# Attention, MLP and gated MLP in one kernel: the opening's order is written out by hand

## The chip, the cores and the metric

The kernel runs on one core of a Trainium2 chip, as one program. The metric is the device time of one execution in microseconds (us). Differences under 0.2% are not told from no change.

## What is computed

Three stages run one after another for a batch of 8, 576 positions and 512 model columns, all in float32:

```python
# 1 attention over 32 memory slots, 8 heads of 64
a = exp(phi - max(phi, axis=2)); a = a / (sum(a, axis=2) + 1e-9)
k_m, v_m = a^T k, a^T v                       # per head: 32 x 64
attn = softmax(q k_m^T / 8);  x = attn v_m    # heads side by side: 576 x 512
# 2 MLP with layer norm, 512 -> 2048 -> 512
x = x + relu(layernorm(x) * g_ln @ w_ch1) @ w_ch2
# 3 gated MLP with a mix over positions
h = gelu(x @ w_in); u, v = halves(h)
out = x + (u * (w_sg @ (layernorm(v) * g) + b_sg)) @ w_out
```

The weights arrive as float64 and are turned into float32 on the chip. A product that needs float32 exactness is made of three matmuls on fp32r parts: high by high, high by low, low by high.

## The kernel before

**Stages.** `phase1` does attention and the first MLP for the eight batches, `phase2` the gated MLP. This change is in the first batch of `phase1`.

**Preparing a batch.** `load_phi`, `load_kv`, `load_rem` and `load_q` fetch phi, k, v and q. The 64 positions past 512 are loaded on their own, as `prz` (phi) and `kvr` (k and v). `prep_red` and `prep_max` find the column maxima, `prep_exp` subtracts and exponentiates, `prep_sum` sums over positions, `prep_kv` makes k_m and v_m (`kvp`), `prep_norm` divides (`kvn`), and `prep_T` turns them (`ptk`, `kvT`).

**Queries.** Three groups of query tiles belong to batch 0: tiles 0 and 1, tiles 2 and 3, and the half tile 4. For each, `t_q` turns q (`ptq`, `qT`), `t_scores` makes scores (`sc`) and their exponentials (`z`), `t_norm` divides, and `t_attn` writes the high and low part of the attention weights (`aTh`, `aTl`). `t_x` makes attention's output (`px`, `x`), which only the residual and the layer norm need.

**W1 and W2.** w_ch1 is used in four quarters of 512 columns, each four raw tiles of 128 x 512 float64. `to_f32` converts a raw tile with one ScalarE and two VectorE instructions (lines 112 to 114). `scale_w1` multiplies by the layer norm's weight (`wc`), `center_w1` takes off the column mean (the matmuls `cm`, then line 510), and `make_vw` and `evict_vw` multiply by v_m (`pvw`, `vw`). w_ch2 is 16 raw tiles; `split_w2` converts each and cuts it into `whl`, the low part on GpSimd.

**The MLP's steps.** A step is `m1`, six matmuls from attention weights and `vw` to hidden columns (`ph`, cut into `hh` and `hl`), and `m2`, six matmuls of 512 columns from those with `whl` into `py`. The first batch has two blocks of positions, of 256 and 320. It takes quarter 0 in steps 0 to 3 (first block) and 4 to 7 (second), quarter 1 in steps 8 to 15, and so on. `m2` follows `m1` by `LAG` = 3 steps.

**Order.** `at_time` files each piece of work under a time in steps, and the list is worked off by time. The tile framework then orders each engine's queue by its own estimate of when work is ready, so that the order in the code is not the order on the engines. All DMAs are issued by SyncE (line 85).

Of the kernel before, what the change touches and what calls it, by code (L numbers as in the profile page):

```python
# [26 lines left out]

@with_exitstack
def fused_kernel(ctx: ExitStack, tc: tile.TileContext, q, k, v, phi, g1, w1, w2, w_in, g2, w_sg, b_sg, w_out, out):
    nc = tc.nc  # L30
# [71 lines left out]

    def to_f32(raw, gate=None):

        words = raw.bitcast(U32).rearrange("p (n two) -> p n two", two=2)
        lo, hi = words[:, :, 0], words[:, :, 1]

        gates = ExitStack()
        for ins in gate or ():
            gates.enter_context(tc.issue_after(ins.ins))  # L110
        with gates:
            A.activation(hi.bitcast(F32), hi.bitcast(F32), AF.Prelu, scale=2.0 ** -112, alpha=-(2.0 ** 32))
            V.tensor_scalar(lo, lo, 29, None, op0=ALU.logical_shift_right)
            V.scalar_tensor_tensor(out=lo, in0=hi, scalar=3, in1=lo, op0=ALU.logical_shift_left, op1=ALU.bitwise_or)
        return lo.bitcast(F32)
# [27 lines left out]
    def phase1():  # L143
# [142 lines left out]
        def prep_sum(b):  # L286
            ph, pr = st["phi", b]
            sm = at.tile([P, H, NM], F32, tag="kvn", name="sm")
            G.tensor_tensor(out=sm, in0=ph[:, :, 0, :], in1=ph[:, :, 1, :], op=ALU.add)
            for c in (2, 3):  # L290
                G.tensor_tensor(out=sm, in0=sm, in1=ph[:, :, c, :], op=ALU.add)
            for g in range(2):
                rows, sub = slice(REM * g, REM * g + REM), slice(4 * g, 4 * g + 4)
# [835 lines left out]
```

## Time and profile before

| | |
|---|---|
| time, median of 3 runs (lowest to highest) | 1200.78 us (1200.47 to 1202.09) |
| the profiled execution: time, span | 1204.2 us, 1202.3 us |
| busy: TensorE (PE), VectorE (DVE), ScalarE (ACT), GpSimd (POOL) | 97%, 58%, 39%, 33% of the span |
| TensorE's mean granted clock | 0.989 of full speed |

The shares are means over the whole span. In the profile, PEclk is the granted clock of TensorE as a share of its full 2.4 GHz, and 0.50 is its other level, 1.2 GHz. "SPq" is SyncE's queue, which issues the DMAs.

### The profile page before, as it was taken

The page shows a single profiled execution, that of the slowest core. Times are in us where ns is not written, and L with a number is a line of the kernel's source. Part 1 is how long each engine was busy: PE and PEld are TensorE (multiplying, and loading weights), DVE is VectorE, ACT ScalarE, POOL GpSimd, SP SyncE. Part 2 cuts the span into 40 slices and gives each one's busy share as a digit, 9 for nine tenths or more (in the row PEclk, how much of TensorE's full clock was granted, in tenths as well). Part 3 has the DMA queues.
Part 4 walks back from the last instruction along what each step waited for, and adds up shares of the span by engine and source line. Part 5 has one row for each costly group of instructions (what it writes and reads, how often), then busy time and mean ns, then how long its engine had stood idle before and what let it go on. Part 6 is the DMA issues. An engine that isn't in the chain of part 4 may idle for free.

```text
span 1202.3 us, 20687 instructions
## 1 busy us (share of the span) xinstructions
PE 1168.9 (97%) x7711; PEld 992.1 (83%) x7711; DVE 692.3 (58%) x1669; ACT 466.6 (39%) x1071; POOL 402.4 (33%) x622
## 2 busy tenths in 40 slices
PE   4899999999999999999999999999999999999998
PEld 2487678888788888788888888889989988998997
DVE  4886765645644645644546445567476377447532
ACT  3754423322322322422333445445444354344430
POOL 2233302311201211201211112456666475566641
PEclk8799999999999999999999999999999999999999
DMA  8976544552341551341400343032240042022201
GB/s 251 382 224 176 154 108 117 139 161 55 102 117 27 151 133 49 102 125 27 124 27 19 107 131 111 27 82 88 81 140 18 19 153 66 2 85 83 79 19 71
DMA packets 198900, 124.14 MB, mean 103 GB/s; under 512 B 93072, under 2 KB 174096, under 8 KB 198800
## 3 DMA queue, kind: packets, MB, share of 16 engines
q1 hardware_dynamic: 198800, 122.82, 35.4%
q8 instruction: 61, 1.00, 0.4%
q14 instruction: 39, 0.32, 0.1%
HBM read 99.72 MB, written 31.33 MB: 109 GB/s over the span
## 4 chain that ended last, share of the span: by engine, by line
PE 88%; DVE 6%; DMA 2%; SPq 1%; issue 1%; ACT 1%; POOL 1%; POOLq 0%; DVEq 0%; ACTq 0%
PE ph L596 16%; PE py L628 11%; PE py L626 11%; PE py L627 10%; PE pvs L1034 8%; PE po L1057 8%; PE pv L925 8%; PE pu L1009 7%; PE pvw L548 2%; SPq L85 1%; PE kvp L321 1%; PE cm L508 1%; PE sc L407 1%; PE px L463 1%; PE px L465 1%
## 5 line engine op out<-in xcount | busy, mean ns | idle before, releaser
L596 PE MATMUL ph<-aTh,vw 128*128 128x320 f32 (+1 forms) x1024 | 248.8, 300 | 3.0 <-DVE hl L583 1.7
L626 PE MATMUL py<-whl,hh 128*128 128x512 f32 x512 | 202.0, 395 | 2.9 <-ACT hh L582 2.9
L596 PEld LDWEIGHTS ph<-aTh,vw 128*128 128x128 f32 x1024 | 178.7, 189 | 30.3 <-issue 9.5
L627 PE MATMUL py<-whl,hh 128*128 128x512 f32 x512 | 201.3, 393 | 0.0
L628 PE MATMUL py<-whl,hl 128*128 128x512 f32 x512 | 182.0, 396 | 0.0
L583 DVE SCALAR_TENSOR_TENSOR hl<-ph,hh 128x256 fp32r<-128x256 f32 x256 | 106.3, 420 | 98.9 <-ACT hh L582 98.3
L582 ACT ACTIVATE hh<-ph 128x256 fp32r<-128x256 f32 x256 | 97.0, 385 | 167.5 <-PE ph L596 121.2
L596 PE MATMUL ph<-aTl,vw 128*128 128x256 f32 (+1 forms) x512 | 152.8, 298 | 0.0
L1034 PE MATMUL pvs<-wsh,vhl 128*128 128x288 f32 x576 | 121.0, 295 | 0.0
L626 PEld LDWEIGHTS py<-whl,hh 128*128 128x128 f32 x512 | 96.1, 188 | 25.3 <-ACT hh L582 6.1
L627 PEld LDWEIGHTS py<-whl,hh 128*128 128x128 f32 x512 | 96.3, 188 | 19.5 <-issue 1.1
L1009 PE MATMUL pu<-yTh,whl 128*128 128x288 f32 x512 | 111.0, 296 | 0.4 <-DVE ug L914 0.4
L596 PEld LDWEIGHTS ph<-aTl,vw 128*128 128x128 f32 x512 | 97.1, 190 | 12.2 <-issue 4.3
L628 PEld LDWEIGHTS py<-whl,hl 128*128 128x128 f32 x512 | 89.9, 189 | 10.9 <-issue 1.6
L1034 PEld LDWEIGHTS pvs<-wsh,vhl 128*128 128x128 f32 x576 | 94.4, 188 | 0.6
L925 PE MATMUL pv<-whl,yTh 128*128 128x512 f32 x288 | 91.0, 396 | 0.0
L1057 PE MATMUL po<-whl,gh 128*128 128x512 f32 x288 | 90.0, 391 | 0.0
L1009 PEld LDWEIGHTS pu<-yTh,whl 128*128 128x128 f32 x512 | 85.4, 189 | 1.9 <-DVE ug L914 0.8
L582 ACT ACTIVATE cr<-ph 128x64 fp32r<-128x64 f32 x128 | 28.5, 225 | 146.9 <-PE ph L596 146.5
L430 POOL TENSOR_TENSOR z<-z,r 128x512 f32<-128x512 f32 (+2 forms) x18 | 17.0, 943 | 180.1 <-DVE r L429 130.5
L1037 POOL TENSOR_TENSOR gt<-gt,ug 128x288 f32<-128x288 f32 x64 | 52.9, 827 | 68.6 <-DVE gt L1036 65.8
L1034 PE MATMUL pvs<-wsl,vhl 128*128 128x288 f32 x256 | 75.6, 295 | 0.0
(154 smaller groups left out, 2226.6 us busy)
## 6 DMA issues: line engine op xcount, KB each, us to landing
raw<-in_moe_w_ch_dram SPq DMA_DIRECT2D x32, 512.0 KB, 7.5
wc<-w_d SPq DMA_DIRECT2D x28, 512.0 KB, 5.7
y_d<-x SPq DMA_DIRECT2D x36, 256.0 KB, 2.3
yt<-y_d SPq DMA_DIRECT2D x36, 256.0 KB, 2.7
yr<-y_d SPq DMA_DIRECT2D x36, 256.0 KB, 2.8
kv<-in_k_dram SPq DMA_DIRECT2D x32, 256.0 KB, 3.9
kv<-in_v_dram SPq DMA_DIRECT2D x32, 256.0 KB, 4.4
out_dram<-yr SPq DMA_DIRECT2D x32, 256.0 KB, 2.0
```

The source lines that it names most:

```text
L548: mm = PE.matmul(ps[g][ms, :], vT[rs_, ms], ws[j // 2][rs_, j % 2, :], start=True, stop=True, skip_group_check=True)
L582: high = A.activation(out_h, src, AF.Relu)
L583: return high, V.scalar_tensor_tensor(out=out_l, in0=src, scalar=0.0, in1=out_h.bitcast(F32), op0=ALU.max, op1=ALU.subtract)
L596: R["ph"] = PE.matmul(ph, w_[:, ks], x[:, g, 0:w], start=(n == 0), stop=(n == 3 * HK - 1))
L626: PE.matmul(py, hh, wh, start=start, stop=False)
L627: PE.matmul(py, hh, wl, start=False, stop=False)
L628: PE.matmul(py, hl, wh, start=False, stop=stop)
L925: PE.matmul(pv, y[:, kc, cs], w, start=(n == 0), stop=(n == 3 * KC - 1))
L1009: PE.matmul(pu, w[:, ds_], y[:, kc, cs], start=(n == 0), stop=(n == 3 * KC - 1))
L1034: PE.matmul(pvs, v_, w_, start=(n == 0), stop=(n == len(ops) - 1))
L1037: G.tensor_tensor(out=gt, in0=gt, in1=ug, op=ALU.mult)
L1057: PE.matmul(po, gg[:, dc, cs], w, start=(n == 0), stop=(n == 3 * KC - 1))
```

## The change

From the first instruction up to the end of quarter 1's `evict_vw`, the order of every queue is the order in a new function `opening`: while `pinned["on"]` is set, each instruction is recorded with `keep_in_program_order`. In that stretch ScalarE issues the loads of `prz`, `kvr` and the layer norm's weight. Batch 0's exponentials are summed by VectorE instead of GpSimd. Query tiles 2 to 4 are loaded behind W1's first quarter and taken behind its preparation. The first eight steps run as four `m1`, four `m2`, then the second block's four. PSUM banks are given out from the list `BANKS`. After it, the old way of ordering goes on from step 8; there the conversions of W2's and W1's remaining tiles have moved somewhat, in time and in what gates them.

```diff
+class Traced:
+    def __getattr__(self, name):
+        f = getattr(self._engine, name)
+        if not self._pinned["on"]:
+            return f
+        return lambda *args, **kw: self._tc.keep_in_program_order(f(*args, **kw))
...
+    def load_small(out_ap, in_ap):
+        return (A if pinned["on"] else SP).dma_start(out=out_ap, in_=in_ap)
...
+            if b == 0:
+                for g in range(2):
+                    rows, sub = slice(REM * g, REM * g + REM), slice(4 * g, 4 * g + 4)
+                    V.tensor_reduce(out=sm[:, sub], in_=ph[:, sub].rearrange("p h c m -> p h m c"), axis=AX.X, op=ALU.add)
+                    V.tensor_tensor(out=sm[rows, sub], in0=sm[rows, sub], in1=prz[rows, g], op=ALU.add)
...
-            gate = st.get("hl", tiles[1 if c == 0 else 3]["tr"])
-            W2[c] = split([raws.pop(("w2", c))], wpool, gate=[gate])
+            W2[c] = split([raws.pop(("w2", c))], wpool, gate=R["relu"])
...
-            at_time((-26.5, -26.2, -2.5, 2.0)[fb], load_w1, fb)
-            at_time((-16.5, -5.0, 3.0, 7.5)[fb], scale_w1, fb)
-            at_time((-16.4, -0.3, 4.6, 9.1)[fb], center_w1, fb)
+        for fb in range(2, NFB):
+            at_time((0.6, 2.0)[fb - 2], load_w1, fb)
+            for j in range(KC):
+                at_time((5.7, 8.5)[fb - 2] + 0.56 * j, scale_w1, fb, j)
+            at_time((7.5, 10.3)[fb - 2], center_w1, fb)
...
+        LEAD, AHEAD = 8, 4
...
+        def opening():
+            ga, gb, gc = FIRST
...
+            load_small(g1c, g1.rearrange("(c p) -> p c", p=P))
+            for i in range(2):
+                load_q(us[i], 0, i)
+            load_w1(0)
+            for i in range(2, 5):
+                load_q(us[i], 0, i)
+            for c in range(AHEAD):
+                load_w2(c)
+            load_w1(1)
...
+            prep_T(0)
+            t_scores(ga)
+
+            W, C = raws.pop(0), [raws.pop(("w2", c)) for c in range(AHEAD)]
+            WC[0] = wc_tiles()
+            rebias(W[0])
+            w0 = join(W[0])
+            t_max(ga)
+            rebias(W[1])
+            scale_tile(0, 0, w0)
+            mean_tile(0, 0)
+            w1_ = join(W[1])
+            t_exp(ga)
+            rebias(W[2])
+            scale_tile(0, 1, w1_)
...
+            t_attn(ga)
+            t_scores(gb)
+            t_split(ga, low=False)
+            rebias(C[0])
+            t_q(gc, 0)
+            make_vw(0, [0])
...
+            c0 = join(C[0])
+            m1(*steps[0][1:])
+            m1(*steps[1][1:])
+            m1_relu(*steps[0][1:])
+            high_w2(0, c0)
+            c1 = join(C[1])
+            m1(*steps[2][1:])
...
+            t_exp(gb)
+            t_max(gc)
+            for n in range(AHEAD):
+                m2(*steps[n][1:], n == 0, False)
+            t_exp(gc)
+            prep_vb(0)
+            t_norm(gb)
...
+            make_vw(0, [1])
+            evict_vw(0, 1)
+
+        pinned["on"] = True
+        opening()
+        pinned["on"] = False
+        assert not BANKS
+        for n in range(LEAD, len(steps) + LAG):
```

**SyncE's queue, the first loads.** Before, from behind the second of the four k and v pairs; `raw1` is W1's first quarter, the numbers tell buffers apart:

```order
L85 DMA kvr_165<-in_v_dram 64x4x64
L85 DMA kv_170<-in_k_dram 128x4x128
L85 DMA kv_170<-in_v_dram 128x4x128
L85 DMA kv_173<-in_k_dram 128x4x128
L85 DMA kv_173<-in_v_dram 128x4x128
L85 DMA q0_206<-in_q_dram 128x8x64 x2
L85 DMA q0_209<-in_q_dram 128x8x64 x2
L85 DMA q0_212<-in_q_dram 64x8x64
L85 DMA raw1_214<-in_moe_w_ch1_dram 128x512
L85 DMA raw1_216<-in_moe_w_ch1_dram 128x512
```

In the changed kernel, from the same place:

```order
L36 DMA kv_165<-in_k_dram 128x4x128
L36 DMA kv_165<-in_v_dram 128x4x128
L36 DMA kv_168<-in_k_dram 128x4x128
L36 DMA kv_168<-in_v_dram 128x4x128
L36 DMA q0_177<-in_q_dram 128x8x64 x2
L36 DMA raw1_180<-in_moe_w_ch1_dram 128x512
L36 DMA raw1_182<-in_moe_w_ch1_dram 128x512
L36 DMA raw1_184<-in_moe_w_ch1_dram 128x512
L36 DMA raw1_186<-in_moe_w_ch1_dram 128x512
L36 DMA q0_188<-in_q_dram 128x8x64 x2
L36 DMA q0_191<-in_q_dram 64x8x64
```

The two `prz` and four `kvr` loads have left this queue (they stand first in ScalarE's), and three of the five query loads now stand behind W1's first quarter.

**TensorE, from the turned k_m and v_m to the first step.** Before:

```order
L358 MATMUL ptk<-ident,kvn 128x128 x2
L382 MATMUL ptq<-ident,q_212 128x64 x4
L407 MATMUL sc<-qT_292,kvT 32x256 x8
L407 MATMUL sc<-qT_305,kvT 32x256 x8
L407 MATMUL sc<-qT_318,kvT 32x64 x8
L508 MATMUL cm<-wc,mcol 128x512 x4
L548 MATMUL pvw<-wc,kvT 32x512 x8
L596 MATMUL ph<-aTh,vw 128x256
```

In the changed kernel:

```order
L36 MATMUL ptk<-ident,kvn 128x128 x2
L36 MATMUL sc<-qT_293,kvT 32x256 x8
L36 MATMUL cm<-wc,mcol 128x512 x3
L36 MATMUL ptq<-ident,q_188 128x128 x8
L36 MATMUL cm<-wc,mcol 128x512
L36 MATMUL sc<-qT_358,kvT 32x256 x8
L36 MATMUL ptq<-ident,q_191 128x64 x4
L36 MATMUL pvw<-wc,kvT 32x512 x8
L36 MATMUL sc<-qT_389,kvT 32x64 x8
L36 MATMUL ph<-aTh,vw 128x256
```

The second and third query group have moved from ahead of `cm` into and behind it.

**VectorE, from the centring of quarter 0 on.** Before (`raw1` again W1, here quarter 1; `raw` is W2):

```order
L510 TENSOR_TENSOR wc_384<-wc_384,cm_402 128x1024
L510 TENSOR_TENSOR wc_385<-wc_385,cm_402 128x1024
L427 TENSOR_REDUCE r0_429<-z0_377 128x4
L447 TENSOR_TENSOR aTl_426<-z0_360,aTh_425 128x2x256
L113 TENSOR_SCALAR raw1_225<-raw1_225 128x512
L113 TENSOR_SCALAR raw1_227<-raw1_227 128x512
L113 TENSOR_SCALAR raw1_229<-raw1_229 128x512
L113 TENSOR_SCALAR raw1_231<-raw1_231 128x512
L113 TENSOR_SCALAR raw_233<-raw_233 128x512
L113 TENSOR_SCALAR raw_235<-raw_235 128x512
L113 TENSOR_SCALAR raw_461<-raw_461 128x512
```

In the changed kernel:

```order
L36 TENSOR_TENSOR wc_324<-wc_324,cm_334 128x1024
L36 TENSOR_TENSOR wc_325<-wc_325,cm_334 128x1024
L36 STREAM_TRANSPOSE z0_329<-z0_329 128x512
L36 STREAM_TRANSPOSE z0_408<-sc_375 128x256
L36 STREAM_TRANSPOSE z0_408<-sc_376 128x256
L36 TENSOR_TENSOR aTl_386<-z0_329,aTh_385 128x2x256
L36 TENSOR_TENSOR vw_398<-pvw_396,vw_398 128x512
L36 TENSOR_TENSOR vw_399<-pvw_397,vw_399 128x512
L36 TENSOR_SCALAR raw_193<-raw_193 128x512
L36 SCALAR_TENSOR_TENSOR raw_193<-raw_193 128x512
L36 SCALAR_TENSOR_TENSOR hl_444<-ph_429,hh_443 128x256
L36 TENSOR_SCALAR raw_195<-raw_195 128x512
```

Before, the conversions of seven raw tiles stood between the centring and `vw`; now `vw` follows the centring, and one W2 tile's conversion stands before each step's `hl`.

## Rows read from the trace of the kernel before

**Rows 1.** Busy time by stretch: start:end, length, engines, PEclk, DMA share, GB/s.

```profile
0.00:60.00 60.00, 37.55 (x252) 21.41 (x253) 39.33 (x85) 32.56 (x62) 14.83 (x27) 0.80 0.94 316
60.00:180.00 120.00, 113.78 (x748) 87.68 (x748) 86.45 (x205) 52.85 (x125) 31.50 (x40) 0.99 0.61 166
```

**Rows 2.** TensorE in order of time: start, length, what, [idle before <- releaser].

```profile
30.77 6.64 PE L508 MATMUL cm<-wc,mcol 128*128 128x512 f32 x8 [5.20 <-ACT wc L502]
39.59 3.06 PE L548 MATMUL pvw<-wc,kvT 64*32 64x512 f32 x16 [2.18 <-DVE wc L510]
43.34 0.58 PE L596 MATMUL ph<-aTh,vw 128*128 128x256 f32 x1 [0.69 <-ACT vw L554]
...
51.60 0.80 PE L596 MATMUL ph<-aTh,vw 128*128 128x256 f32 x2
...
73.81 0.68 PE L596 MATMUL ph<-aTh,vw 128*128 128x256 f32 x1
```

**Rows 3.** VectorE in order of time, around quarter 0's centring.

```profile
38.35 2.31 DVE L510 TENSOR_TENSOR wc<-wc,cm 128x1024 f32<-128x1024 f32 x2
...
41.38 2.43 DVE L113 TENSOR_SCALAR raw<-raw 128x512 uint32<-128x512 uint32 x7
...
43.80 4.30 DVE L114 SCALAR_TENSOR_TENSOR raw<-raw 128x512 uint32<-128x512 uint32 x7
...
48.10 1.26 DVE L555 TENSOR_TENSOR vw<-pvw,vw 128x512 fp32r<-128x512 f32 x2
```

**Rows 4.** SyncE's queue in order of time: the issue of the small loads.

```profile
4.02 1.99 SPq L85 DMA_DIRECT2D prz<-in_phi_dram  x2
...
8.69 0.60 SPq L85 DMA_DIRECT2D kv<-in_k_dram  x1
```

**Rows 5.** VectorE in order of time, the preparation of batch 0.

```profile
9.14 0.61 DVE L256 TENSOR_TENSOR pm<-pm,prz 64x128 f32<-64x128 f32 x2 [3.62 <-DMA prz<-in_phi_dram]
...
18.00 0.42 DVE L305 TENSOR_REDUCE rs<-ptsum 128x2 f32<-128x256 f32 x1 [4.71 <-PE ptsum L303]
...
18.93 0.61 DVE L341 TENSOR_SCALAR kvn<-kvp,rs 128x128 f32<-128x128 f32 x2
```

**Rows 6.** Short stretches, columns as in rows 1: the DMAs, and TensorE's clock.

```profile
8.00:10.00 2.00, 0.52 (x2) 0.36 (x2) 0.59 (x3) 0.00 (x0) 0.00 (x0) 1.00 0.60 131
12.00:14.00 2.00, 1.28 (x25) 1.03 (x28) 1.25 (x4) 1.72 (x4) 0.29 (x1) 1.00 0.99 252
16.00:18.00 2.00, 2.00 (x34) 1.47 (x27) 0.00 (x1) 0.00 (x0) 0.95 (x3) 1.00 0.92 208
50.00:51.00 1.00, 1.00 (x3) 0.48 (x2) 0.97 (x3) 0.02 (x1) 1.00 (x2) 0.81 1.03 422
```

**Rows 7.** ScalarE in order of time: the last raw tile of quarter 0.

```profile
28.14 0.70 ACT L112 ACTIVATE raw<-raw 128x512 f32<-128x512 f32 x1 [0.57 <-DMA raw<-in_moe_w_ch_dram]
```

**Rows 8.** The chain that ended last, single links: start, length, what.

```profile
65.94 0.47 PE py L628 x2
...
68.82 0.88 PE ph L596 x6
...
79.43 0.71 PE ph L596 x6
...
108.75 3.43 PE cm L508 x8
```

**Rows 9.** Busy time on one tile: TensorE on py, px, cm, then VectorE on z.

```profile
43.00:73.81 30.81, 10.60 (x40) 0.88 0.88 289
...
43.00:73.81 30.81, 5.46 (x24) 0.88 0.88 289
...
43.00:73.81 30.81, 8.09 (x14) 0.88 0.88 289
...
0.00:60.00 60.00, 12.71 (x23) 0.80 0.94 316
```

**Rows 10.** The page's costliest groups: one of VectorE.

```profile
L583 DVE SCALAR_TENSOR_TENSOR hl<-ph,hh 128x256 fp32r<-128x256 f32 x256 | 106.3, 420 | 98.9 <-ACT hh L582 98.3
```

More of the change, by code (lines that the diff above doesn't have):

```diff
@@ L111, in to_f32 @@
         with gates:
[L112 to L115, printed above, removed]
+            rebias(raw)
+            return join(raw)
     def split(raws, wp, scale=None, gate=None):
@@ L154, in phase1 @@
         VBs = [[at.tile([P, 2, 4 * D], F32R, name=f"VB{n}{i}") for n in "hl"] for i in range(2)]
+        prz = at.tile([P, 2, 4, NM], F32, name="prz")
+        G.memset(prz, 0.0)
         for i in range(2):
@@ L288, in prep_sum @@
             sm = at.tile([P, H, NM], F32, tag="kvn", name="sm")
[L289 to L293, printed above, removed]
-                G.tensor_tensor(out=sm[rows, sub], in0=sm[rows, sub], in1=prz[rows, g], op=ALU.add)
+            if b == 0:
[3 more added lines that the diff above has]
+                    V.tensor_tensor(out=sm[rows, sub], in0=sm[rows, sub], in1=prz[rows, g], op=ALU.add)
+            else:
+                G.tensor_tensor(out=sm, in0=ph[:, :, 0, :], in1=ph[:, :, 1, :], op=ALU.add)
+                for c in (2, 3):
+                    G.tensor_tensor(out=sm, in0=sm, in1=ph[:, :, c, :], op=ALU.add)
+                for g in range(2):
+                    rows, sub = slice(REM * g, REM * g + REM), slice(4 * g, 4 * g + 4)
+                    G.tensor_tensor(out=sm[rows, sub], in0=sm[rows, sub], in1=prz[rows, g], op=ALU.add)
             st["sm", b] = sm
-            if b < 2:
+            if b == 1:
                 turn_sum(b)
@@ L445, in t_attn @@
                 ah, al = (x[:, :, c0:c0 + m] for x in aT_of(j))
-                A.copy(ah, src)
-                lo = (V if 0 < t0 <= TB and b == 0 else G).tensor_tensor(out=al, in0=src, in1=ah.bitcast(F32), op=ALU.subtract)
-            for u in us:
-                u["T"]["tr"] = tr if t0 == 0 else lo
+                if high:
+                    A.copy(ah, src)
+                if low:
+                    (G if b else V).tensor_tensor(out=al, in0=src, in1=ah.bitcast(F32), op=ALU.subtract)
         def t_x(gr, i):
@@ L597, in m1, with m1_relu @@
                     n += 1
+            st["ph", j, c] = ph
+            if not pinned["on"]:
+                m1_relu(j, c)
+        def m1_relu(j, c):
+            ph = st.pop(("ph", j, c))
+            b, t0, t1, _, _ = blocks[j]
+            w = t1 - t0
             hh = mo.tile([P, 2 * P], F32R, tag="hh", name="hh", bufs=LAG + 1)
@@ L647, in phase1 @@
         }
+        FIRST = []
         last_q = [-99.0, -99.0]
```

254 lines of the change are left out of this document (180 added, 74 removed).

## The prediction

> **What bounds the kernel now.** I read the stretches first. From 60 to 180 us TensorE is idle for 6.2 us of 120, but in the first 60 us for 22.5, and its granted clock there is 0.80 on average [rows 1]. So the engine that bounds the kernel is lost in the opening, and what the change can win is won there. The order of time then shows how: the column means `cm` start at 30.77, the products `pvw` at 39.59, the first step's `ph` at 43.34, and TensorE comes back to it only at 51.60 [rows 2]. In that gap VectorE converts seven raw tiles, from 41.38 to 48.1, before it makes the low part of `vw` that the step needs [rows 3].
>
> **The point of comparison** is the first matmul of step 8. It starts at 73.81 before [rows 2]. The two kernels have not done the same work by then. Until 73.81 the old one did 40 of the 48 `py` matmuls that the new one does ahead of step 8, 14 `cm` matmuls where the new one has 8, and 24 `px` matmuls, of which the new one does 12 [rows 9]. A `py` matmul takes 0.235 us, six 256-column ones 0.71, eight `cm` 3.43 [rows 8]. The old kernel would have had the new one's work done at 73.81 + 8 x 0.235 - 6 x 0.43 - 12 x 0.118 = 71.7 us.
>
> **1. Small loads and sums, up to `kvn`.** Six small loads held SyncE's queue from 4.02 to 8.69 [rows 4]; the maxima waited 3.62 us for `prz`, until 9.14 [rows 5], and in 8 to 10 us the DMA engines were only 0.60 busy [rows 6]. On ScalarE's queue the issue costs ScalarE some 5 us in which it has nothing else to do. The maxima cannot come before 9.14 - 3.62 = 5.5; I take 5.9. The other arm is data: phi, k, v and the small loads are 2.94 MB, at 252 GB/s [rows 6] 11.7 us, so about 13.5 us if DMA starts near 2 us (an estimate). Then come half of the `kvp` matmuls, the turned sums, and the 1.54 us from 18.00 to the end of `kvn` [rows 5], some 2.8 us in all. `kvn` is ready at 16.3 instead of 19.54, 3.2 us earlier, whichever arm I take. VectorE's summing costs it about 2.5 us (two reductions like those of the maxima and two additions), all while the k and v still land; with that cover gone it would cost those 2.5.
>
> The Trainium skill (DMA: Bandwidth & Descriptors, Issuing engines are not separate DMA queues) says that DMAs of several engines run on the same 16 DMA engines, so that only issue time is saved. By that rule this step gives nothing where the engines were full, and the sum would be up to 3.2 us smaller; the share of 0.60 says that they were not.
>
> **2. W1's first quarter.** Its last raw tile was taken at 28.14, on landing [rows 7]. Two query tiles (0.52 MB) now stand ahead of it instead of five. At the 208 GB/s of query loads [rows 6] they land at 13.5 + 2.5 = 16.0. The quarter's 2.1 MB take 5.0 us at 422 GB/s, the rate of a later stretch [rows 6], or up to 7.2, the time that it took before, behind the five query tiles (2.94 MB at 252 and 1.18 at 208 GB/s from 2 us on, and some 1.5 us starved, end near 21). That is 21 to 23.2; I take 22.
>
> **3. Centring.** Before, it began 10.2 us after the last tile (38.35) [rows 3, 7]. Now three ScalarE passes, a VectorE pair and the wait behind the first group's exponentials lie between, about 3.7 us, so the last scaled tile is there at 25.7. TensorE must then do two `cm` tiles and eight turns of queries. At the lower clock a `cm` matmul takes 6.64 / 8 = 0.83 us [rows 2], the turns about 2. That gives 27.7 at the full clock and 31 at the lower one; I take 30.0, nearer the latter, since TensorE has had gaps before. So 8.3 us are gained here.
>
> **4. First step.** Before, `ph` began 5.0 us after the centring [rows 2, 3]. ScalarE now has a cast, a conversion and a copy in front of `vw`, VectorE two transposes. I take 5.2: 35.2 us. The low part of `vw` follows at 36.2, no longer at 48.1.
>
> **5. Four steps with four W2 tiles.** VectorE does per step a raw tile (6.73 us for seven, 0.96) [rows 3] and an `hl` of 0.42 [rows 10]: 5.5 us, up to 41.7. Then come the exponentials of the second and third group: `z` took VectorE 12.71 us in all three [rows 9]; these two hold 640 of the 1152 columns, 7.1 us, less 0.7 for transposes already done, and their low parts add some 1.1: 7.5, and 0.4 for the last cast. The second block's first step can start at 49.6. TensorE's own arm: four steps until 40.3, then 24 `py`, half of them at half speed, 8.5 us, until 48.8. VectorE decides, narrowly.
>
> **6. The second block's four steps.** 4 x 0.88 + 12 x 0.118 + 24 x 0.235 + 3.43 [rows 8] and `pvw`, which took 3.06 at the lower clock with a wait inside [rows 2], so some 1.2: 15.2 us of TensorE. VectorE has four raw tiles, four `hl`, the centring (2.3) and `vw` in the same time, about 12. With 0.5 for the first `vw`, step 8 starts at 65.3. The lead is 71.7 - 65.3 = 6.4 us.
>
> **7. What is given back.** By the place of step 8 the old kernel had converted six raw tiles more (quarter 2, and two of W2); the new one owes them, 6 x 0.96 = 5.8 us of VectorE. VectorE has room, 33.5 idle us from 60 to 180 [rows 1], but the first is urgent: W2's tile 4 now waits for step 8's `hl`. Its path is a step's matmuls (0.7), `hh` and `hl` (0.8), conversion and cast (2.3) and one or two instructions queued between (0.4 to 1.3), 4.2 to 5.1. TensorE has four steps and two output tiles to do meanwhile, 4 x 0.71 + 1.4 = 4.2. So nothing to 0.9 is lost, and as much at the second tile. With the fuller queues of step 8 to 16 I take 2.0, bounds 0 and 5.8. GpSimd's low parts of W2 lie beside it, its queue being empty.
>
> Steps past 16 have TensorE as bound in both. So the sum is 6.4 - 2.0 = 4.4 us. The profiled execution took 1204.2 us and the median of the runs is 1200.8; the difference is the profile's, so I take the 4.4 off the median: **1196.4 us**.
>
> **Rivals.** *The lead is kept and larger.* If the clock is back by the centring (27.7 in step 3), W1 lands at 21 and nothing is given back, the lead is 10 to 11: 1190. For it: VectorE is the limit in few places. Against it: every hand-worked wait is a best case.
>
> *It is all given back.* Steps 8 to 16 need two quarters' conversions at once. If the six owed tiles cost their full 5.8, 0.6 is left: 1200. For it: VectorE's 28% of idle from 60 to 180 lies mostly late. Against: each tile is needed only a step after the last.
>
> *Slower: the clock.* In 50 to 51 us, busy throughout, TensorE still had a granted clock of 0.81 [rows 6], between its two levels of 1.2 and 2.4 GHz. The new steps come with gaps, for each `m1` waits for the `hl` of two steps before. From step 0 to step 8 TensorE has 24 us of work at full speed, of which the sum lets 6 run at half. Each further one costs 1 us where TensorE is waited for. From 4.4 further ones on the change loses; if the 15 us of step 6 also ran at half, step 8 would start at 80, and the kernel would take 1211.
>
> The Trainium skill (TensorE: Matmul & The Clock Gate, What's actually happening) has the clock throttled by default and released by activity. The trace agrees: 0.80 in the first 60 us, 0.99 after. By that rule alone gaps between the new steps speak against the change.
>
> **Numbers.** Forecast 0.47 (1193.5 to 1198.3); larger lead 0.20; given back, within 0.2% (2.4 us, about what a measurement can tell) 0.20; slower 0.13, the clock or a queue that I misread. The range takes in the larger lead down to 1188.5 and the slower case up to 1203; a tenth is left out on either side. Faster 0.67, same 0.20, slower 0.13.
>
> **What would show it.** `kvn` near 16.3, the last raw tile of quarter 0 near 22, centring near 30, step 0 near 35, the second block's first step near 50 and step 8 near 65. A clock still at 0.5 past 50 us, or idle of TensorE above 5 us between steps 8 and 16, would make it wrong; so would `kvn` later than 18, or W1 no earlier than 25.

## The result, and the profile of the changed kernel

The changed kernel is slower: 1214.44 us median of 4 runs (1213.33 to 1216.09), against 1200.63 (1200.47 to 1202.09) for the kernel before on the same chip. The ratio is 1.0113, with a 95% interval of 1.0096 to 1.0131; 1196.4 had been predicted. The profiled execution of the changed kernel took 1213.48 us (span 1211.7). That of the kernel before lay 3.6 us above its median, so the two traces differ by 9.3 us where the medians differ by 13.8; the traces can say where the 9.3 went.

Busy time by stretch of the changed kernel, columns as in [rows 1]:

```profile
0.00:60.00 60.00, 37.45 (x266) 24.38 (x266) 41.96 (x87) 25.75 (x52) 11.48 (x22) 0.91 0.97 310
60.00:180.00 120.00, 107.71 (x682) 79.79 (x682) 85.03 (x196) 58.47 (x132) 32.58 (x40) 0.94 0.60 165
```

The first 60 us are better only in the clock (0.91 for 0.80). From 60 to 180 us TensorE is now idle for 12.3 us where it was 6.2, and its clock has fallen from 0.99 to 0.94. The loss lies behind the opening. TensorE in order of time (line 36 is the wrapper that keeps the order, so it stands for all lines of the opening):

```profile
35.48 0.39 PE L36 MATMUL ph<-aTh,vw 128*128 128x256 f32 x1
...
52.68 0.58 PE L36 MATMUL ph<-aTh,vw 128*128 128x320 f32 x1 [3.65 <-ACT aTh L36]
...
72.07 0.39 PE L644 MATMUL ph<-aTh,vw 128*128 128x256 f32 x1 [0.73 <-ACT vw L36]
...
99.91 0.33 PE L332 MATMUL ptsum<-ident,sm 128*128 128x128 f32 x1 [1.23 <-POOL sm L323]
100.08 3.60 PE L549 MATMUL cm<-wc,mcol 128*128 128x512 f32 x8
...
106.16 1.08 PE L350 MATMUL kvp<-kv,phi 128*32 128x128 f32 x32 [2.38 <-issue]
...
108.21 1.96 PE L597 MATMUL pvw<-wc,kvT 64*32 64x512 f32 x16 [0.75 <-DVE pvw L588]
110.89 0.58 PE L644 MATMUL ph<-aTh,vw 128*128 128x256 f32 x1 [0.71 <-ACT vw L603]
```

Step 0 starts at 35.48 instead of 43.34, step 4 (the 320-column block's first) at 52.68, step 8 at 72.07. Then the last five rows: quarter 2's `cm` runs only at 100.08, between the two turned sums (`ptsum`) of the second batch, its `pvw` stands behind that batch's `kvp`, and step 16 starts at 110.89. Between steps 8 and 16 TensorE was idle for 8.35 us, where the kernel before, which has other work in that stretch, was idle for 1.18; as stretches, the changed kernel first:

```profile
72.07:110.89 38.82, 30.47 (x185) 22.38 (x185) 29.96 (x61) 20.65 (x43) 14.51 (x16) 0.91 0.62 172
```

```profile
73.81:96.69 22.88, 21.70 (x126) 17.01 (x125) 20.87 (x46) 13.65 (x30) 7.58 (x9) 1.00 0.71 201
```

ScalarE had made quarter 2's last scaled tile long before its `cm`:

```profile
91.83 0.76 ACT L539 ACTIVATE wc<-raw,g1c 128x512 f32<-128x512 f32 x1 [0.46 <-DVE raw L129]
```

In the kernel before, the same `pvw` ran at 82.64, ahead of the second batch's `ptsum` and `kvp`, and step 16 started at 96.69; its TensorE in order of time:

```profile
82.64 1.09 PE L548 MATMUL pvw<-wc,kvT 64*32 64x512 f32 x16
...
104.09 0.27 PE L303 MATMUL ptsum<-ident,sm 128*128 128x128 f32 x1
104.29 0.63 PE L321 MATMUL kvp<-kv,phi 128*32 128x128 f32 x12
```

VectorE, ScalarE and GpSimd of the changed kernel in order of time, in the opening:

```profile
6.06 0.28 DVE L36 TENSOR_TENSOR pm<-pm,prz 64x128 f32<-64x128 f32 x1 [1.38 <-DMA prz<-in_phi_dram]
...
16.54 0.61 DVE L36 TENSOR_SCALAR kvn<-kvp,rs 128x128 f32<-128x128 f32 x2
...
24.52 0.69 ACT L36 ACTIVATE raw<-raw 128x512 f32<-128x512 f32 x1
...
30.49 2.35 DVE L36 TENSOR_TENSOR wc<-wc,cm 128x1024 f32<-128x1024 f32 x2 [2.75 <-PE cm L36]
...
38.52 0.69 DVE L36 SCALAR_TENSOR_TENSOR raw<-raw 128x512 uint32<-128x512 uint32 x1
...
38.60 3.25 POOL L36 TENSOR_TENSOR whl<-raw,whl 128x512 fp32r<-128x512 f32 x2 [35.15 <-ACT whl L36]
...
39.46 1.20 DVE L36 TENSOR_SCALAR raw<-raw 128x512 uint32<-128x512 uint32 x1
40.77 1.63 DVE L36 SCALAR_TENSOR_TENSOR raw<-raw 128x512 uint32<-128x512 uint32 x1
...
43.44 1.66 DVE L36 SCALAR_TENSOR_TENSOR raw<-raw 128x512 uint32<-128x512 uint32 x1
```

The first four places answer to [rows 5, 7, 3]: maxima, `kvn`, the last raw tile of quarter 0 and its centring. The rest are step 5's conversions: those beside a GpSimd subtraction take 1.20 us in place of 0.42, and 1.63 and 1.66 in place of 0.69.

### The profile page after: what moved, and what is told of

Read it like the earlier page. It is cut to its first block, busy times and chain, and to the rows that moved or that the text cites. A ratio compares the mean times of both kernels' runs of the same rounds, so it can differ in the third digit from the quotient of the medians.

```text
span 1211.7 us, 20696 instructions
## 1 busy us (share of the span) xinstructions
PE 1170.3 (97%) x7711; PEld 992.7 (82%) x7711; DVE 701.0 (58%) x1674; ACT 466.9 (39%) x1071; POOL 400.9 (33%) x616
## 3 DMA queue, kind: packets, MB, share of 16 engines
q1 hardware_dynamic: 196640, 122.49, 35.2%
## 4 chain that ended last, share of the span: by engine, by line
PE 86%; DVE 7%; DMA 3%; ACT 1%; issue 1%; POOL 1%; SPq 0%; POOLq 0%; DVEq 0%; ACTq 0%
PE ph L644 16%; PE py L682 10%; PE py L684 10%; PE py L683 10%; PE pvs L1236 8%; PE po L1259 8%; PE pv L1127 8%; PE pu L1211 7%; PE pvw L597 2%; PE kvp L350 1%; DVE raw L36 1%; PE sc L436 1%; PE px L505 1%; PE px L507 1%; PE px L506 1%
## 5 line engine op out<-in xcount | busy, mean ns | idle before, releaser
L644 PE MATMUL ph<-aTh,vw 128*128 128x320 f32 (+1 forms) x992 | 240.4, 301 | 2.4 <-ACT vw L36 0.7
L682 PE MATMUL py<-whl,hh 128*128 128x512 f32 x496 | 195.2, 397 | 5.4 <-ACT hh L630 2.6
L644 PEld LDWEIGHTS ph<-aTh,vw 128*128 128x128 f32 x992 | 173.3, 190 | 27.1 <-issue 6.6
L683 PE MATMUL py<-whl,hh 128*128 128x512 f32 x496 | 195.1, 394 | 0.0
L684 PE MATMUL py<-whl,hl 128*128 128x512 f32 x496 | 176.7, 396 | 0.0
L631 DVE SCALAR_TENSOR_TENSOR hl<-ph,hh 128x256 fp32r<-128x256 f32 x248 | 103.1, 422 | 99.9 <-ACT hh L630 99.2
L630 ACT ACTIVATE hh<-ph 128x256 fp32r<-128x256 f32 x248 | 94.2, 385 | 172.4 <-PE ph L644 125.6
L644 PE MATMUL ph<-aTl,vw 128*128 128x320 f32 (+1 forms) x496 | 147.6, 298 | 0.0
L682 PEld LDWEIGHTS py<-whl,hh 128*128 128x128 f32 x496 | 93.1, 188 | 28.1 <-ACT hh L630 5.3
L683 PEld LDWEIGHTS py<-whl,hh 128*128 128x128 f32 x496 | 93.6, 189 | 18.2 <-issue 0.5
L644 PEld LDWEIGHTS ph<-aTl,vw 128*128 128x128 f32 x496 | 94.4, 190 | 9.5 <-issue 1.7
L1211 PE MATMUL pu<-yTl,whl 128*128 128x288 f32 x256 | 75.5, 295 | 0.0
```

The source lines that it names most:

```text
L630: high = A.activation(out_h, src, AF.Relu)
L631: return high, V.scalar_tensor_tensor(out=out_l, in0=src, scalar=0.0, in1=out_h.bitcast(F32), op0=ALU.max, op1=ALU.subtract)
L644: R["ph"] = PE.matmul(ph, w_[:, ks], x[:, g, 0:w], start=(n == 0), stop=(n == 3 * HK - 1))
L682: PE.matmul(py, hh, wh, start=start, stop=False)
L683: PE.matmul(py, hh, wl, start=False, stop=False)
L684: PE.matmul(py, hl, wh, start=False, stop=stop)
```

## The experiments

Ratios are to the kernel before, run on the same chip; an interval of 95% follows in brackets. Differences in us between two experiments are of their medians, mostly from different chips, so the ratios are the safer measure. Steps are counted in `ph` matmuls, six to a step; their starts, in us of each trace. The trace of the kernel before comes from an execution 3.6 us above the median, so a lead over it in this table can be that much too large:

| | step 0 | 4 | 8 | 16 | 24 | 48 | ratio |
|---|---|---|---|---|---|---|---|
| before | 43.3 | 59.5 | 73.8 | 96.7 | 125.0 | 207.5 | 1 |
| changed | 35.5 | 52.7 | 72.1 | 110.9 | 139.9 | 214.5 | 1.0113 |
| old_times | 34.3 | 51.5 | 70.6 | 101.9 | 135.6 | 214.3 | 1.0089 |
| w2_early | 35.4 | 52.6 | 73.1 | 109.6 | 136.6 | 211.0 | 1.0078 |
| unpinned | 33.2 | 56.4 | 66.5 | 103.8 | 135.5 | 209.7 | 1.0065 |
| unpinned_old | 33.0 | 56.9 | 66.5 | 96.5 | 125.1 | 206.3 | 1.0026 |
| small_only | 36.5 | 52.2 | 64.4 | 88.1 | 118.1 | 196.9 | 0.9948 |
| small_gates | 37.3 | 51.4 | 63.5 | 90.7 | 122.6 | 201.1 | 0.9982 |
| small_times | 36.7 | 50.9 | 62.4 | 108.9 | 136.3 | 210.7 | 1.0082 |
| small_behind_q2 | 36.5 | 50.6 | 62.1 | 93.2 | 128.7 | 203.8 | 1.0032 |

### In the changed kernel: old times, two owed tiles, half the order, a busy TensorE

**old_times** puts W1's quarters 2 and 3, and W2's tiles 4 to 7, back in the list; when quarter 2 is loaded, and what the tiles wait for (their gates), stay as changed:

```diff
-                at_time((5.7, 8.5)[fb - 2] + 0.56 * j, scale_w1, fb, j)
-            at_time((7.5, 10.3)[fb - 2], center_w1, fb)
-            at_time((8.0, 11.0)[fb - 2], make_vw, 0, [fb])
+                at_time((3.0, 7.5)[fb - 2], scale_w1, fb, j)
+            at_time((4.6, 9.1)[fb - 2], center_w1, fb)
+            at_time((5.8, 10.3)[fb - 2], make_vw, 0, [fb])
...
-            at_time(split_at + (0.6 if c < 8 else 0), split_w2, c)
+            at_time(split_at, split_w2, c)
```

> The changed kernel, with quarters 2 and 3 of W1 and W2's tiles 4 to 7 put back to the times that they had before (scale at 3.0 and 7.5, centring at 4.6 and 9.1, vw at 5.8 and 10.3, no 0.6 added). Theory A (the loss comes after step 8, because quarter 2 is made ready just in time: its pvw starts at 108.21, before it was 82.64): the waits of TensorE from 105 to 118 us shrink, and the time falls from 1214.4 by 4 to 8 us, to about 1208. Rival B (the clock falls whenever VectorE is late, whatever is late) and rival C (the loss was made inside the kept order, by step 8): less than 2.4 us of change, 1212 to 1217. If it comes out slower than 1217, the retiming was a remedy and not a cause.

It took 1211.25 us, 1.0089 [1.0072, 1.0106]: some 3 us better, less than theory A asked and more than its rivals allowed, and the interval overlaps that of the changed kernel. TensorE in order of time shows what came in place of the old wait:

```profile
79.38 2.08 PE L549 MATMUL cm<-wc,mcol 128*128 128x512 f32 x2 [4.01 <-ACT wc L539]
...
93.25 1.09 PE L597 MATMUL pvw<-wc,kvT 64*32 64x512 f32 x16
...
112.35 0.61 PE L644 MATMUL ph<-aTh,vw 128*128 128x320 f32 x1 [2.28 <-DVE hl L631]
```

`pvw` comes 15 us sooner, but now TensorE waits 4.01 us for the quarter's scaled tiles between steps 8 and 12, and later 2.28 us for an `hl`.

**w2_early** loads W2's tiles 4 and 5 in `opening` and converts them around quarter 1's centring (`rebias(C4)`, `join(C4)`, `high_w2(4, c4)`, and the same for 5).

> The changed kernel, with W2's tiles 4 and 5 loaded behind W1's second quarter and converted inside the kept order, around the centring of quarter 1, where VectorE is idle for 2.0 and 1.95 us (65.6 to 67.6, 70.1 to 72.05). Theory A (what is owed at step 8 is the loss): the two raw tiles, 2 x 0.96 us of VectorE and a wait of 1.71 for the low part at 79.28, are gone from behind step 8; 1209 to 1212, some 2.5 to 5 us faster than the changed kernel. Rival C (the order inside the opening is the loss): VectorE has more to do there, step 8 comes later by 1 to 2 us, and the time stays at 1213 to 1216.

1210.14 us, 1.0078 [1.006, 1.0096]: as theory A expected, although step 8 came 1.0 us later, as C expected. At steps 24 and 48 it is 3.3 and 3.5 us ahead of the changed kernel.

**half_pinned** stops keeping the order at `t_exp(gb)`.

> The changed kernel with its order kept only up to the fourth W2 tile of the opening; from the second query group's exponentials to step 8 the scheduler orders the queues. Rival C (the hand-written order of that half costs: step 4 at 52.68 in place of the 49.6 worked out, and step 8 at 72.07 in place of 65.3): step 8 comes 3 to 5 us earlier, the time is 1207 to 1211. Theory A (the loss is behind step 8): within 2.4 us of 1214.4.

1212.62 us, 1.0104 [1.0089, 1.0119]: no difference that this can show, as theory A expected, though step 8 came at 70.3. Step 3 started at 46.1 instead of 39.6; the kept order is better there and worse behind it.

**warm** adds 14 matmuls that nobody reads, behind the four `m2`:

```diff
+            for _ in range(14):
+                PE.matmul(warm, W2[3][0][:, 0:P], W2[3][0], start=True, stop=True)
```

> The changed kernel with 14 more matmuls of 512 columns, whose result nobody reads, behind the first four m2, so that TensorE is not idle for the 3.65 us ahead of step 4. Rival B (the lower clock after that wait costs): steps 4 and 5 run at the full clock, 1.6 us are won up to step 8, and if the clock stays up behind it as well, 3 to 5 us of the total, 1209 to 1212. Theory A: the 1.6 us go into waiting for VectorE, 1212.5 to 1215.5.

1210.2 us, 1.0082 [1.0067, 1.0097], inside rival B's range. The two steps behind TensorE's wait, first in the changed kernel and then here, as stretches:

```profile
52.68:56.10 3.42, 3.42 (x12) 3.33 (x13) 0.92 (x4) 1.13 (x3) 0.00 (x0) 0.51 1.06 328
```

```profile
51.23:54.70 3.47, 3.47 (x24) 3.33 (x25) 1.65 (x5) 1.64 (x4) 0.00 (x0) 1.00 1.04 339
```

After 3.65 us of idle the granted clock was 0.51 and 3.42 us held 12 matmuls; with TensorE kept busy it was 1.00, and 3.47 us held 24. Step 4 to step 8 took 17.5 us instead of 19.4. So the low clock costs 1.9 us up to step 8. The rest of the gain is not told apart from the start of this trace, which was 1.45 us ahead at step 0 already, before the added matmuls.

### Two owed causes at once, the order not kept, one part alone, the low parts on VectorE

**w2_four_old**: `old_times`, and W2's tiles 4 to 7 all converted inside the kept order.

> The changed kernel with W2's tiles 4 to 7 converted inside the kept order (tile 4 ahead of quarter 1's centring, the others behind it and beside pvw), and with quarters 2 and 3 and W2's later tiles at the times of the kernel before. Theory A (the loss is work owed at step 8 that meets the preparation of quarter 2 and of the second batch on VectorE between 75 and 105 us): the two partial remedies, 1.85 us for the old times and 3 us for two tiles, add up or more, since both serve the same queue; 1204 to 1208, TensorE's idle from 75 to 120 us down from 7.3 to under 4. Rival D (no more than a shift: the stretch with too little work for TensorE moves to another place, as it did with the old times): 1208 to 1212.

1209.73 us, 1.008 [1.0063, 1.0096]. The remedies do not add. Step 8 moved to 74.2, and step 16 stood at 102.3, near the 101.9 of the old times alone. The time is in rival D's range and outside A's.

**unpinned** leaves all else as changed, but keeps no order:

```diff
-        if not self._pinned["on"]:
+        if not self._pinned["keep"]:
             return f
```

> The changed kernel with the order not kept: the scheduler orders the opening's queues by its own estimates; the loads, sums, steps and later times are the changed ones. Rival C (the hand-written order itself loses): faster than 1214 by 4 us or more, 1202 to 1210. Theory A (the order is not at fault, what is owed behind it is): the opening is worse than with the order kept, VectorE converts W1's second quarter or W2 early as in the kernel before, and the time stays at 1210 to 1222.

1208.64 us, 1.0065 [1.005, 1.008]: rival C is right for this part, about 5.8 us. Step 4 comes 3.8 us later than with the order kept, step 8 5.6 us sooner. From step 4 to step 8, TensorE's stretch without and with the kept order:

```profile
56.44:66.50 10.06, 10.06 (x69) 8.26 (x68) 4.67 (x12) 3.88 (x11) 0.00 (x0) 1.00 0.95 304
```

```profile
52.68:72.07 19.39, 17.57 (x85) 12.37 (x85) 11.16 (x28) 8.25 (x19) 2.10 (x5) 0.91 0.91 253
```

The scheduler had VectorE prepare quarter 1 ahead of step 4; the written order does it in these four steps, where each step's `hl`, a raw tile and the next step wait for one another. The quarter's centring on VectorE, without and with the kept order:

```profile
53.95 2.35 DVE L553 TENSOR_TENSOR wc<-wc,cm 128x1024 f32<-128x1024 f32 x2
```

```profile
67.61 2.35 DVE L36 TENSOR_TENSOR wc<-wc,cm 128x1024 f32<-128x1024 f32 x2 [2.00 <-PE cm L36]
```

That this is where the 5.8 us come from is not shown: in `half_pinned` the same centring was at 57.62, and the total was no better.

**small_only** is the kernel before with the small loads of batch 0 on ScalarE:

```diff
+    def load_small(b, out_ap, in_ap):
+        return (nc.sync if b else nc.scalar).dma_start(out=out_ap, in_=in_ap)
...
-        at_time(-26.3, lambda: load(g1c, g1.rearrange("(c p) -> p c", p=P)))
+        at_time(-26.3, lambda: load_small(0, g1c, g1.rearrange("(c p) -> p c", p=P)))
```

(`prz` and `kvr` likewise, and `prz`'s memset first.)

> The kernel before with one part of the change alone: the memset of prz first, and batch 0's loads of prz, kvr and the layer norm's weight issued by ScalarE. The prediction's step 1 (kvn 3.2 us earlier) holds by itself: kvn at 16 to 17.5 in place of 18.93 in the trace. Whether that reaches the end: W1's first quarter bounds the centring in the kernel before (its last raw tile was taken at 28.14 on landing), and SyncE's queue now reaches the W1 loads 2 to 4 us earlier. If it reaches the end: 1196 to 1199; if the seven raw tiles ahead of vw and the clock take it: within 2.4 us of the kernel before.

1194.41 us, 0.9948 [0.993, 0.9966]: faster than both kernels, and than the 1196 to 1199 expected. Its lead of 6.8 us at step 0 in the traces is not given back: 9.4 at step 8, 10.6 at step 48. `kvn` started 2.2 us sooner, at 16.72, but `cm` 7.0 us, at 23.73. The view of the tile `g1c`, the layer norm's weight, in the kernel before shows what else was late:

```profile
L502 ACT ACTIVATE wc<-raw,g1c x4: 739/745/753, 30.0 to 32.5; 128x512 f32<-128x512 f32 x4
L85 SPq DMA_DIRECT2D g1c<-in_moe_g_ln_dram x1: 881/881/881, 21.3 to 21.3; - x1
...
DMA to landing us min/median/max: 8.3/8.3/8.3
```

Its 2 KB were issued at 21.3, behind five raw tiles of W1, and landed 8.3 us later, at 29.6; the first scaled tile `wc` follows at 29.96, though the first raw tile was converted at 25.7. In `small_only`, ScalarE in order of time:

```profile
6.65 0.49 ACTq L88 DMA_DIRECT2D g1c<-in_moe_g_ln_dram  x1
...
22.03 0.75 ACT L505 ACTIVATE wc<-raw,g1c 128x512 f32<-128x512 f32 x1
```

That the weight alone makes the gain was not tried: the last raw tile, too, was taken sooner (24.51, before 28.14).

**low_on_v** makes the opening's four low parts of W2 with `V.tensor_tensor` in place of `G.tensor_tensor`.

> The changed kernel with the opening's four low parts of W2 made on VectorE in place of GpSimd. If VectorE's conversions of 39 to 45 us were stretched by GpSimd's work beside them (1.20, 1.63 and 1.66 us where 0.42 and 0.69 are usual), they fall back to 0.42 and 0.69 from step 0 to step 4, which gives back about 2.7 us, and the four subtractions cost VectorE some 4 x 0.6: step 4 within 1 us of its 17.2 us behind step 0, the time within 2.4 us of 1214.4. If the stretch has another cause, the durations stay, and step 4 comes 2 to 3 us later.

1215.97 us, 1.013 [1.0115, 1.0145], no different from the changed kernel. VectorE in order of time:

```profile
42.84 0.69 DVE L36 TENSOR_TENSOR whl<-raw,whl 128x512 fp32r<-128x512 f32 x1
43.45 0.42 DVE L36 TENSOR_SCALAR raw<-raw 128x512 uint32<-128x512 uint32 x1
43.91 0.69 DVE L36 SCALAR_TENSOR_TENSOR raw<-raw 128x512 uint32<-128x512 uint32 x1
```

With GpSimd idle every conversion is back at 0.42 and 0.69, so GpSimd's subtractions had stretched them, by 0.78 + 0.94 + 0.97 = 2.7 us. The four subtractions, 2.8 us, take the same from VectorE: step 4 came 18.4 us behind step 0, not 17.2, a little more than the 1 us expected.

### From the fast version back to the slow one

**small_times** adds to `small_only` the change's later times (those that `old_times` undid, and quarter 2's load at 0.6 instead of -2.5 and its store at 8.6) and its gate `R["relu"]` on these tiles.

> The kernel before with the small loads on ScalarE (1194.4 us in an earlier run, 0.52% faster than before), and now with the changed kernel's later times as well: W1's third quarter loaded at 0.6 and scaled from 5.7, its vw at 8.0, the fourth at 8.5 and 11.0, W2's tiles 4 to 7 at 0.6 later, all waiting for the last step's hl. Theory E (the later times are the loss: quarter 2 is made ready just in time, beside the second batch's preparation): pvw of quarter 2 comes 15 us or more later than in that kernel, TensorE gets idle between steps 8 and 24, and the time is 1199 to 1207. Theory F (the loss comes from the opening's own shape, in which steps stand ahead of conversions and six tiles are owed at step 8; the times only follow): within 3 us of 1194.4.

1209.32 us, 1.0082 [1.0067, 1.0097]: 14.9 us slower than `small_only` (1.35% by the ratios), with step 8 even 2.0 us sooner. Theory F falls; E holds in kind, but the loss is larger than its 1199 to 1207. The same `pvw` in `small_only`, then TensorE of `small_times` in order of time, and a stretch of it:

```profile
79.24 1.09 PE L551 MATMUL pvw<-wc,kvT 64*32 64x512 f32 x16
```

```profile
93.86 0.47 PE L306 MATMUL ptsum<-ident,sm 128*128 128x128 f32 x1 [7.10 <-POOL sm L297]
94.12 6.37 PE L511 MATMUL cm<-wc,mcol 128*128 128x512 f32 x8
...
103.09 1.94 PE L324 MATMUL kvp<-kv,phi 128*32 128x128 f32 x32 [2.49 <-issue]
...
106.20 1.96 PE L551 MATMUL pvw<-wc,kvT 64*32 64x512 f32 x16 [0.75 <-DVE pvw L542]
```

```profile
80.00:100.00 20.00, 12.90 (x42) 8.09 (x41) 7.74 (x17) 6.99 (x13) 6.98 (x8) 0.74 0.55 148
```

```profile
80.31 0.77 ACT L505 ACTIVATE wc<-raw,g1c 128x512 f32<-128x512 f32 x1
```

Quarter 2's last scaled tile was there at 81.08, as this row of ScalarE shows. But its `cm` stands behind `ptsum` in TensorE's queue, and that waits 7.10 us for GpSimd's sums. These could start only at 88.57, behind the second batch's exponentials, and two low parts of W2, 2.6 us, run between them. Then `cm` runs at a granted clock of 0.56 (6.37 us, where 3.43 is usual [rows 8]). `kvp`, ahead of `pvw`, waits 2.49; the trace names no releaser, but VectorE's centring had ended 0.2 us before it started. VectorE is busy for 7.74 us of 20: nobody is short of capacity. Quarter 2's later load is not what held it up: no conversion from 62 us on waited for a transfer.

**unpinned_old** is `unpinned` with the old times.

> The changed kernel with the order not kept (1208.6 us in an earlier run) and the later times of the kernel before. Theory E (the later times are the loss): 1196 to 1203, for its step 8 came at 66.5 us, 7 us ahead of the kernel before. Theory F (the owed tiles are the loss whenever they are made): 1205 to 1210, with the wait moved from steps 16 to 24 to steps 8 to 16, as the old times alone did with the order kept (1211.3).

1203.23 us, 1.0026 [1.0015, 1.0038]: 5.4 us better than `unpinned` (0.39%), just past the upper end of E's range and better than F's.

**small_sums** and **small_sums_q** add to `small_only` VectorE's summing, then the later query loads:

```diff
-                        at_time(-27, load_q, us[i], ub, qi)
+                        at_time(-27 if tt < 2 else -26.4, load_q, us[i], ub, qi)
```

> The kernel before with the small loads on ScalarE and the first batch's exponentials summed on VectorE. The unpinned kernel, which has both, has its kvn at 14.55 to 15.5 us, small loads alone at 16.72: so kvn at 14.5 to 15.5. If the opening's lead is kept to the end, as with the small loads, 1 to 2 us faster than 1194.4; if W1's first quarter (its first raw tile landed at 20.5 there) is what centring waits for, within 2.4 us of it.

> As the last one, and query tiles 2 to 4 loaded behind W1's first quarter, the scheduler ordering the rest. W1's first raw tile lands some 2 to 4 us earlier than 20.5, the centring (33.85 at its end there) comes as much earlier if the scheduler puts the second query group behind it. If it does, 2 to 4 us faster than small_sums; if it keeps the three groups' scores ahead of the centring, the late queries hold it up, and the time is the same or up to 3 us slower.

`small_sums`: 1194.75 us, 0.9958 [0.9943, 0.9972], no different from `small_only`; `kvn` at 15.5, 1.2 us sooner, buys nothing: quarter 0's centring came later, at 34.06 instead of 31.50. `small_sums_q`: 1200.44 us, 1.0002 [0.9993, 1.0012], 5.7 us lost, more than the 3 expected. TensorE and then VectorE in order of time:

```profile
23.18 2.01 PE L391 MATMUL ptq<-ident,q 128*128 128x128 f32 x8 [3.86 <-DMA q<-in_q_dram]
...
31.02 5.51 PE L517 MATMUL cm<-wc,mcol 128*128 128x512 f32 x8 [1.51 <-DVE z L425]
```

```profile
38.49 2.34 DVE L519 TENSOR_TENSOR wc<-wc,cm 128x1024 f32<-128x1024 f32 x2
```

W1 lands sooner (first raw tile at 17.68), but the scheduler keeps the late queries ahead of `cm`, and the centring slips from 34.06 to 38.49. The change's written order avoids just that, with its centring at 30.49, 1.0 us sooner than that of `small_only`.

### What in the later times costs

**small_behind_q2** is `small_times` with the second batch's `ptsum` and first `kvp` filed behind quarter 2's `pvw`:

```diff
+            if b == 1:
+                at_time(8.05, turn_sum, b)
...
-                    at_time(pb + kv_at[g] * f, prep_kv, b, [g])
+                    at_time((8.1, pb + kv_at[1] * f)[g] if b else pb + kv_at[g] * f, prep_kv, b, [g])
```

> The small loads and the changed later times (1209.3 us in an earlier run), and one thing more: the second batch's turned sums (ptsum) and first half of kvp are filed behind quarter 2's pvw, at 8.05 and 8.1, in place of 6.5 and 7.9. Theory G (the later times put quarter 2's cm behind ptsum, which waits for GpSimd's sums, and its pvw behind kvp, which waits for the bank that cm holds): the waits of 7.10 and 2.49 us ahead of ptsum and kvp are gone, pvw of quarter 2 starts before 98 us in place of 106.2, and the time is 1196 to 1202. Rival H (quarter 2 as such is too late, whatever stands ahead of it): 1206 to 1210.

1203.69 us, 1.0032 [1.0019, 1.0044]: 5.6 us better, between G and H. TensorE in order of time:

```profile
84.83 3.60 PE L511 MATMUL cm<-wc,mcol 128*128 128x512 f32 x8
...
91.38 1.09 PE L551 MATMUL pvw<-wc,kvT 64*32 64x512 f32 x16 [1.57 <-DVE pvw L542]
94.01 0.41 PE L306 MATMUL ptsum<-ident,sm 128*128 128x128 f32 x2
...
107.70 1.93 PE L324 MATMUL kvp<-kv,phi 128*32 128x128 f32 x32 [4.34 <-DMA kv<-in_v_dram]
```

Both waits are gone and `pvw` runs at 91.38, not 106.20. A part comes back as a wait of 4.34 us: the second half of `kvp` needs k and v, whose loads SyncE issued only from 101.35 on, behind nine query loads.

**behind_q2** and **behind_q2_w2** do the same in the changed kernel, without and with W2's tiles 4 to 7 in the opening.

> The changed kernel (1214.4 us) with the same: the second batch's ptsum and first kvp filed behind quarter 2's pvw. Theory G: the waits of 1.23 (ptsum), 2.38 (kvp), 0.75 (pvw) and part of the lower clock of 110 to 118 us go; 1206 to 1210. Rival H (there VectorE is the late one: it converts quarter 2's last raw tile only at 101 us, so cm cannot come earlier): 1211 to 1216.

> The same, with W2's tiles 4 to 7 converted inside the kept order as well, at the later times of the change. If VectorE's debt at step 8 and the order of TensorE's queue are two causes, they add: 3 us or more faster than with the order of the queue alone, 1202 to 1207. If they are one, no more than 1.5 us apart.

1210.2 us, 1.0087 [1.0068, 1.0107], and 1211.31 us, 1.0092 [1.0074, 1.011]. The first is 3 to 4 us better than the changed kernel, between the 1206 to 1210 of theory G and the 1211 to 1216 of rival H, and its interval overlaps that of the changed kernel. H's premise was a misreading: in the changed kernel quarter 2's last scaled tile was there at 92.59, and the one at 101 us is quarter 3's first (in `behind_q2` the last `cm` of quarter 2 starts at 96.14, ahead of that tile). The owed tiles add nothing to it.

**small_gates** is `small_only` with the change's gates and the 0.6 for W2's tiles 4 to 7, quarters 2 and 3 at their old times.

> The small loads alone (1194.4 us) with the change's gates only: W2's tiles 4 on and W1's third and fourth quarter wait for the last step's relu and hl, and W2's tiles 4 to 7 are 0.6 later; quarters 2 and 3 stay at their old times. Theory G: the gates do little, 1193 to 1198. If the gates hold the conversions back until their step, and the later times only follow: 1202 or more.

1198.13 us, 0.9982 [0.9971, 0.9994], just past G's range and far from its rival's 1202: 0.34% of the 1.35%.

**small_w2_sooner** and **small_q2_sooner** move the same two groups 0.6 sooner.

> The kernel before with the small loads on ScalarE (1194.4 us, ratio 0.9948), and W2's tiles 4 to 7 converted 0.6 sooner in place of 0.6 later. If lateness alone costs (the gates and the 0.6 cost 0.34%), sooner is as good or better: ratio 0.991 to 0.995. If the old times are a balance, in which each queue's order shifts with any move, it is slower, 0.996 to 1.002: the second batch's ptsum then stands earlier in TensorE's queue, too.

> The same kernel with W1's third and fourth quarter scaled, centred and turned into vw 0.6 sooner, the W2 tiles at their old times. If lateness alone costs (the later times cost 1.0%): ratio 0.991 to 0.995. If the old times are a balance: 0.996 to 1.002, the conversions of W2's tiles 4 to 7 being pushed behind the quarter's, and TensorE waiting for a whl.

1195.64 us, 0.9964 [0.9951, 0.9977], and 1195.94 us, 0.9967 [0.9956, 0.9978]: not told apart from `small_only`, and not better. Both lie at the near edge of the range for a balance (0.996 to 1.002) and outside that for lateness alone (0.991 to 0.995), but so close to `small_only` that a balance is not shown; moving these groups 0.6 sooner gains nothing.

## Why the prediction was wrong

**Steps 1 to 4 held.** `kvn` was ready at 17.15 (16.3 predicted), the last raw tile was taken at 24.52 (22), the centring began at 30.49 (30.0) and step 0 at 35.48 (35.2). But these steps never named a wait that the trace of the kernel before shows, for the layer norm's weight until 29.6. The Trainium skill (DMA: Bandwidth & Descriptors, Issuing engines are not separate DMA queues) says that other issuing engines save only issue time, usually little. Here seven small loads gained 0.52% (`small_only`); how much of it is issue time, and how much their place in the queue, no run separates.

**Step 5 was 2.8 us short.** It had VectorE through at 49.6; step 4 began at 52.68, of which 0.3 came from step 0. Conversions were priced at 0.96 a tile; beside GpSimd they stretched by 2.7. `low_on_v` shows the cause of the stretch. The error was to price GpSimd's low parts at nothing for VectorE: step 7 says that they "lie beside it, its queue being empty". The Trainium skill (SBUF — State Buffer, Who interferes with whom) has a VectorE instruction with two SBUF inputs, or in a two-port mode, wait for a whole GpSimd instruction that reads SBUF and was issued first; the trace agrees (0.69 to 1.63 and 1.66).

**Step 6 was 3.7 us short.** Step 4 to 8 took 19.39 us, not 15.7. TensorE was busy for 17.57 instead of 15.2; 1.7 of that are the two steps at clock 0.51 (3.42 less 2 x 0.88). And it was idle for 1.8, in waits for `hl`, `wc` and `vw`, of which the sum had 0.5. So step 8 came at 72.07, and the lead over the equal-work 71.7 was gone: -0.4 instead of 6.4.

**Step 7 is the one that decided.** It gave back 2.0 (bounds 0 to 5.8); in the traces (by their spans) it was 9.4 - 0.4 = 9.0, in the medians 13.8 - 0.4 = 13.4. Of the 18.2 us between the forecast and the median, steps 5 and 6 make 6.8 and this step 11.4. It priced six owed tiles on VectorE (by 73.81 the kernel before had converted 17, the changed one 12 by its step 8, so five) and called TensorE the bound past step 16. The prediction's own sign of being wrong came out: TensorE idle for 8.35 us between steps 8 and 16, against the 5 that it named. It did not price a thing that the diff showed: quarter 2's preparation filed at 5.7 to 8.0 instead of 3.0 to 5.8, where the second batch's `ptsum` and `kvp` are filed. `small_times` shows it as sufficient for a loss of this size: in the kernel before's own opening, with step 8 sooner, these times and gates cost 14.9 us. Of them `small_behind_q2` gets back 5.6 by the order of TensorE's queue, and `small_gates` loses 3.7 by gates and W2's tiles alone; if the two add, which was not tried, 5.6 remain, and what makes them stays open. In the changed kernel undoing the times gives back only some 3 us; TensorE then waits between steps 8 and 12. There the causes overlap, and their gains do not add (`w2_four_old`, `behind_q2_w2`).

**The kept order** costs 5.8 us (`unpinned`), which the prediction nowhere had as a cost.

**One way to divide the loss.** Six runs can be read as a chain in which each holds the parts of the one before it and more. The ratio goes from 1 to 0.9948 with the small loads, 0.9958 with VectorE's sums, 1.0002 with the late queries (in the scheduler's order), 1.0026 with the rest of the change at the old times and its order not kept (`unpinned_old`), 1.0065 with the later times (`unpinned`) and 1.0113 with the order kept. So the queries cost 0.44%, the later times 0.39% and the kept order 0.48%, each known to about 0.2%. The shares hold for this order of adding alone: in `small_times`, where the gates come with them, the later times cost 1.35%.

**The rivals.** The slower one, the clock, named the right side but not the cause: the low clocks stand behind waits (0.51 behind 3.65 us here, 0.56 behind 7.10 us in `small_times`), and 1.9 us up to step 8 are shown. Its chance of 0.13 covered "a queue that I misread" as well, which is nearer, without saying which queue. The larger lead was added up too high: 2.3 for the centring and 1.0 for W1 on top of 6.4 make 9.7, not 10 to 11.

What stays open: which waits make up the 13.8 us, since only 9.3 of them lie in the traces; what in the kept order costs; and whether a written order with the scheduler's early quarter 1 would keep the lead.

## What to carry to other kernels

When a change moves work later, look up what is filed at the new place for the same engine queue, and for the same banks: an instruction that is ready waits behind one that is not. A lead worked out up to one step is worth nothing until the work that the new kernel owes there has been placed as well. And test the parts of a large change alone: here the small loads were the only part that was shown to gain.
